# Strassen's scheme for the second projection of a fused retention and snake-activation kernel

## The chip, the cores and the metric

The kernel runs on one core of a Trainium2 chip. A core has five engines that each work through their own queue in order: TensorE (PE; its weight loads are shown apart as PEld), VectorE (DVE), ScalarE (ACT), GpSimd (POOL) and SyncE (SP, which here only issues DMAs). TensorE writes its results to PSUM, which has eight banks; the other operands live in SBUF. The metric is the device time of one execution in microseconds, the median of the runs.

## The reference

Eight batches of retention (attention with a decay instead of a softmax) give 4608 rows of 512 features, and a feed-forward layer with a snake activation maps these rows to the output. Cut to what is computed:

```python
scores = scale * np.matmul(q, k.transpose(0, 1, 3, 2))        # 8 batches, 8 heads, 576 positions, 64 features
ret = scores * Dmat[None, :, :, :]                            # gamma[h] ** (i - j) below the diagonal, 0 above
attn_out = np.matmul(ret, v)
x = attn_out.transpose(0, 2, 1, 3).reshape(B * S, H * D)      # 4608 x 512
h = x @ w_in                                                  # 512 -> 2048
s = np.sin(alpha * h)
g = h + s * s / (alpha + 1e-09)
out = g @ w_out                                               # 2048 -> 512
```

## The kernel before

The 4608 rows are worked on in nine blocks of 512 rows. Blocks 0 to 7 are the first 512 positions of batches 0 to 7; block 8 gathers the last 64 positions of all eight. The output features 2048 of the first projection are cut into sixteen chunks of 128, and a chunk of one block is called a unit here.

One unit (lines 541 to 573): `project(n, u, tag)` runs four matmuls of 128 x 128 x 512 into one PSUM bank `hps`; `sine` (ScalarE) writes `s`; `square` (ScalarE or VectorE, or in a few early places GpSimd) writes `ss`; `product` (VectorE) writes the chunk `gT[n][:, u, :]`, 128 features by 512 rows, in 16-bit floats, and with it the bank is free. In the steady part the banks rotate through three tags, `h0`, `h1` and `h2`, so the projection of unit u + 3 waits for the product of unit u. `gT` has two buffers, one for the block that is being made and one for the block that is being consumed.

The second projection of block n - 1 runs between the units of block n: `gemm2(n - 1, u, tag)` (line 587) is four matmuls of 128 x 128 x 512, that is, 128 of the block's 512 rows against four of the sixteen chunks of `w_out16`. Four such calls fill the bank `op`; `finish` (line 581) copies it to `osb` on ScalarE and stores it with two DMAs from SyncE's queue. A block takes 64 such matmuls.

Blocks 0 to 2 and the beginning of the attention are written out call by call. From line 1140 a loop over n = 3 to 8 writes the order. In each turn of it, called iteration n below, unit u = 0 to 15 does in this order: `project`, `sine`, the calls in `todo[u]`, `square`, `product`, `gemm2`, and the calls in `after[u]`. `at_unit(u, ...)` fills `todo`, `behind(u, ...)` fills `after`. What is placed there is the attention of batch n + 1 (called `A`):

- `scores` at units 3 and 8 into the two double banks `m0` and `m1`, each used twice; `masked` on VectorE behind units 3, 4, 8 and 9 (line 380), which frees the double bank;
- `values` and `add_states` at unit 12, in which the second half of the matmuls waits for a mark that passes through GpSimd's queue (`relay=G_`); `keep` on ScalarE;
- for batch n + 2: loads from SyncE's queue, casts on GpSimd (lines 121 and 194) at units 3 to 8, transposes by DMA from SyncE's queue at units 13 and 15, and the sums of the states (`outer` at unit 12, `chain` on GpSimd).

Iterations 7 and 8 have no such attention; iteration 7 has the small part for block 8 (`Ends`). After the loop, lines 1221 to 1230 run the second projection of block 8: 64 matmuls, of which the last 16 are cut into 320 and 192 columns so that the last copy and store are short.

SBUF is full, so tiles rotate through numbered buffers whose order is written out in the table `BUFFERS`, one digit for each use; `place` takes the next digit.

## Time and profile before

| | us |
|---|---|
| median of 3 runs | 305.76 |
| lowest and highest run | 305.32, 308.21 |
| span of the profiled execution (first to last instruction) | 303.7 |
| TensorE busy in it | 293.0 |
| ScalarE busy | 193.6 |
| VectorE busy | 188.7 |
| GpSimd busy | 136.1 |

The profiled execution's own time is not listed apart from its span; the median of the runs is 2.06 us above the span, and this difference is taken as what lies around it. Iteration n in this text lasts from the start of its first projection to that of the next iteration; the first projections of iterations 4 to 8 start at 136.46, 167.3, 198.2, 228.37 and 258.45 us of the span, and the loop's last matmul ends at about 286.1.

### The profile page before, as it was taken

What the parts mean: (1) busy time and instruction counts of PE and PEld (TensorE: products, weight loads), DVE (VectorE), ACT (ScalarE), POOL (GpSimd) and SP (SyncE); (2) the same over time, 40 slices, a digit from 0 to 9 for tenths busy, and PEclk for the clock granted to TensorE, in tenths of its full rate; (3) what the DMA queues carried; (4) which work ended last, traced back from release to release, by engine and by line L of the source; (5) the groups of instructions that cost most, each with busy time, mean ns of one, the idle gap of its engine ahead of it and who ended that gap; (6) DMA issues with size and microseconds to landing.
All of it is one profiled execution on the core that took longest, in us unless ns stands there. A gap on an engine that the chain in (4) does not pass through costs nothing.

```text
span 303.7 us, 7880 instructions
## 1 busy us (share of the span) xinstructions
PE 293.0 (96%) x3208; PEld 156.8 (52%) x3208; DVE 188.7 (62%) x280; ACT 193.6 (64%) x322; POOL 136.1 (45%) x151
## 2 busy tenths in 40 slices
PE   5899999999989999999999999999999999999995
PEld 4666545645445544554455444544555454444443
DVE  2587876878257776667665666666666755555500
ACT  1569935996776978665776577756764556555411
POOL 4693579482888766587076517743030000000000
PEclk9599999999999999999999999999999999999999
DMA  8999999998798679899788979956451121111232
GB/s 216 349 226 214 259 291 321 227 266 224 169 228 186 149 174 215 236 157 169 166 241 127 183 174 273 171 130 164 103 109 39 41 43 38 37 35 35 47 90 73
DMA packets 120484, 50.05 MB, mean 165 GB/s; under 512 B 80384, under 2 KB 115456, under 8 KB 120448
## 3 DMA queue, kind: packets, MB, share of 16 engines
q1 hardware_dynamic: 116928, 45.17, 63.8%
q0 software_dynamic: 2688, 4.19, 7.6%
q8 instruction: 25, 0.41, 0.5%
q10 hardware_dynamic: 832, 0.18, 0.4%
q14 instruction: 11, 0.09, 0.1%
HBM read 36.75 MB, written 9.44 MB: 152 GB/s over the span
## 4 chain that ended last, share of the span: by engine, by line
PE 84%; DMA 8%; ACT 4%; SPq 1%; issue 1%; POOL 0%; DVE 0%; POOLq 0%; ACTq 0%; DVEq 0%
PE hps L549 38%; PE ops L592 36%; DMA raw<-in_v_dram 5%; PE o L414 3%; PE sc L372 2%; PE kv L308 2%; DMA qT<-q 2%; DMA raw<-in_k_dram 1%; PE o L436 1%; ACT v L119 1%; SPq L143 1%; PE idle L605 1%; ACT kT L119 1%; SPq L585 0%; PE tr L227 0%
## 5 line engine op out<-in xcount | busy, mean ns | idle before, releaser
L573 DVE SCALAR_TENSOR_TENSOR gT<-ss,inva,hps 128x512 f16<-128x512 f16 x144 | 106.1, 746 | 64.0 <-ACT ss L566 59.0
L592 PE MATMUL ops<-w_out,gT 128*128 128x512 f16 (+2 forms) x592 | 142.5, 374 | 0.1
L557 ACT ACTIVATE s<-hps,alpha_t 128x512 f16<-128x512 f32 x144 | 97.5, 684 | 67.3 <-PE hps L549 65.3
L549 PE MATMUL hps<-xT,w_in 128*128 128x512 f16 (+1 forms) x532 | 126.1, 371 | 0.2 <-ACT xT L119 0.2
L549 PEld LDWEIGHTS <-w_in 128*128 128x128 f16 x596 | 66.7, 114 | 57.9 <-DMA w_in<-in_moe_w_in_dram 0.3
L592 PEld LDWEIGHTS <-gT 128*128 128x128 f16 x592 | 56.1, 98 | 62.3 <-issue 0.4
L566 ACT ACTIVATE ss<-s 128x512 f16<-128x512 f16 x73 | 45.9, 631 | 1.4
L568 DVE TENSOR_TENSOR ss<-s 128x512 f16<-128x512 f16 x63 | 32.2, 512 | 19.9 <-ACT s L557 19.4
L194 POOL TENSOR_TENSOR k<-raw,cn 128x1024 f16<-128x1024 f32 (+1 forms) x17 | 29.4, 1733 | 25.9 <-DMA raw<-in_k_dram 25.5
L119 ACT COPY osb<-ops 128x512 f32<-128x512 f32 (+1 forms) x34 | 19.7, 580 | 16.2 <-PE ops L592 14.9
L194 POOL TENSOR_TENSOR q<-raw,cn 128x1024 f16<-128x1024 f32 x13 | 24.6, 1902 | 3.7 <-DMA raw<-in_q_dram 2.7
L384 DVE TENSOR_TENSOR ret<-sc,mask 128x1024 f16<-128x1024 f32 x16 | 19.2, 1221 | 3.0 <-PE sc L372 3.0
L354 POOL TENSOR_TENSOR kvs<-s,kvs 128x256 f32<-128x256 f32 x21 | 16.4, 780 | 4.2 <-ACT kvs L119 1.9
L549 PE MATMUL hps<-xS,w_in 128*128 128x512 f16 x64 | 16.4, 379 | 0.0
L353 POOL TENSOR_TENSOR s<-kvs,cn 128x256 f32<-128x256 f32 x21 | 12.8, 611 | 6.6 <-ACT kvs L119 6.5
L121 POOL CAST v<-raw 128x1024 f16<-128x1024 f32 x10 | 10.5, 1056 | 11.2 <-DMA raw<-in_v_dram 8.5
L384 DVE TENSOR_TENSOR ret<-sc,mask_halved 128x768 f16<-128x768 f32 x16 | 15.2, 951 | 0.0
L178 POOL TENSOR_TENSOR ks<-ks,cn 128x512 f16<-128x512 f32 x4 | 4.2, 1042 | 21.9 <-DMA vs<-in_v_dram 11.6
L119 ACT CAST xT<-o 128x1024 f16<-128x1024 f32 (+1 forms) x15 | 12.9, 878 | 1.1 <-PE o L436 1.0
L346 POOL TENSOR_TENSOR s<-kvs,cn 128x256 f16<-128x256 f32 x17 | 10.8, 635 | 5.8 <-ACT kvs L119 3.4
L372 PEld LDWEIGHTS <-kT 64*64 64x64 f16 x512 | 7.7, 110 | 8.5 <-issue 8.0
L372 PE MATMUL sc<-qT,kT 64*64 64x128 f16 (+1 forms) x512 | 10.7, 219 | 1.2 <-DMA qT<-q 1.1
(58 smaller groups left out, 149.2 us busy)
## 6 DMA issues: line engine op xcount, KB each, us to landing
out_dram<-osb SPq DMA_DIRECT2D x70, 128.0 KB, 2.7
raw<-in_q_dram SPq DMA_DIRECT2D x16, 512.0 KB, 5.4
raw<-in_k_dram SPq DMA_DIRECT2D x8, 512.0 KB, 6.1
raw<-in_v_dram SPq DMA_DIRECT2D x8, 512.0 KB, 7.9
raw<-in_v_dram SPq DMA_DIRECT2D x32, 128.0 KB, 3.0
raw<-in_k_dram SPq DMA_DIRECT2D x32, 128.0 KB, 3.2
w_in<-in_moe_w_in_dram POOLq DMA_DIRECT2D x4, 512.0 KB, 11.5
w_out<-in_moe_w_out_dram POOLq DMA_DIRECT2D x4, 512.0 KB, 12.8
```

The lines of the kernel that those rows point to most:

```text
L119: eng.copy(d_, s_)
L194: eng.tensor_tensor(dst[:, a0:a1].rearrange("p a r t d -> p t (a r) d"), t_.rearrange("p (t a) x -> p t a x", t=2)[:, :, a0:a1].rearrange( ...
L353: nc.gpsimd.tensor_tensor(s32, self.kvs[:, c - 1], g1.unsqueeze(2).to_broadcast([P, 4, D]), MULT)
L354: nc.gpsimd.tensor_tensor(self.kvs[:, c], s32, self.kvs[:, c], ADD)
L372: matmul(sc[halves(g), t, c : c + n], kT[halves(t), 2 * a + r, halves(g)], qT[halves(t), 2 * a : 2 * a + 2, 64 * g + i0 : 64 * g + 64], st ...
L384: nc.vector.tensor_tensor(ret.rearrange("p t (z x) -> p (t z) x", z=2)[:, :, 0:n], sc.rearrange("p t (z x) -> p (t z) x", z=2)[:, :, 0:n], ...
L549: matmul(hps_of[n, fc][0][:, cols], w_in16[fc // 4][:, a, fc % 4 :: 4], xs[n][:, a, cols], start=(a == 0 and part != 1), stop=(a == KT - 1 ...
L557: nc.scalar.activation(s_t, hps, mybir.ActivationFunctionType.Sin, bias=0.0, scale=alpha_t[:, fc : fc + 1],)
L566: nc.scalar.activation(ss_t, s_t, mybir.ActivationFunctionType.Square)
L568: eng.tensor_tensor(ss_t, s_t, s_t, MULT)
L573: nc.vector.scalar_tensor_tensor(gT[n][:, fc, :], ss_t, inva[:, fc : fc + 1], hps, MULT, ADD)
L592: matmul(ops[n, c, cols.start][:, cols], gT[n][:, fk, c * P : (c + 1) * P], w_out16[:, fk, cols], start=(fk == 0), stop=(fk == FC - 1), sk ...
```

## The change

For blocks 3 to 8 the second projection no longer runs as 64 matmuls of 512 columns. The 512 rows are cut into two halves t, the 2048 features into two halves h (chunks 0 to 3 and 8 to 11 for h = 0, the others for h = 1; the index p tells which of the two groups of four chunks), and the 512 output columns into two halves e. Strassen's scheme, in Winograd's form, makes the 2 x 2 product of these quarters from seven products instead of eight. One product (`part_product`) is 16 matmuls of 128 x 128 x 256 into one bank. Their factors are quarters or sums of quarters:

- on the weights, once: `T3`, `T2` and `T4` behind units 5 to 10 of iteration 3, and `T1`, in place in `w_out16`, behind units 2 and 4 of iteration 4, all on VectorE (128 x 1024 each, eight instructions);
- on the rows, for each block: `S3` (in place in `gT`) and `S2` on VectorE, `S1` and `S4` on GpSimd, two halves p of each, 128 x 1024 each. `S3` and `S2` of p = 0 come behind units 11 and 15 of the block's own iteration, those of p = 1 behind units 0 and 1 of the next, and all of `S1` and `S4` behind unit 1 of the next.

The results are put together by ScalarE and VectorE (`after_product`): the first and second product are copied by ScalarE, the five others are added by VectorE to a kept tile (128 x 512, 32 bit) before two stores. Products 2, 7 and 3 accumulate in the bank of products 1, 6 and 5.

The loop's units run in pairs in iterations 4 to 8: both projections of a pair, then one product, with its `after_product` ahead of the second unit's square and product. Iteration 3 keeps the old order (`plain`), since block 2 is still projected as before. Squares are dealt out anew between VectorE and ScalarE, `masked(0, 1)` and the second `scores` move by a unit, casts start one unit later, and two `raw` buffers, and some others, are given to the sums. After the loop, block 8's seven products and eight row sums run in a row.

```diff
@@ BUFFERS
-    "raw": "012345012345012345102405314023140253401253401253",
-    "k16": "0123012302130213",
-    "q16": "0120120121201201",
+    "raw": "012345012345012345102405314023140240124012401240",
+    "k16": "0123012302131313",
+    "q16": "0120120121202020",
...
+    def weight_sum(name, p, eng):
+        b11, b12, b21, b22 = (w_quarter(h, e, p) for h in range(2) for e in range(2))
+        out_, x, y, op = {
+            "T1": lambda: (b12, b12, b11, SUB),
+            "T2": lambda: (piece("T2", p), piece("T3", p), b11, ADD),
+            "T3": lambda: (piece("T3", p), b22, b12, SUB),
+            "T4": lambda: (piece("T4", p), b21, piece("T2", p), SUB),
+        }[name]()
+        eng.tensor_tensor(out_, x, y, op)
+
+    def row_sum(n, name, p, eng):
+        a11, a12, a21, a22 = (quarter(n, t, h, p) for t in range(2) for h in range(2))
+        out_, x, y, op = {
+            "S1": lambda: (piece("S1", p), a11, piece("S2", p), ADD),
+            "S2": lambda: (piece("S2", p), a22, a21, SUB),
+            "S3": lambda: (a21, a11, a21, SUB),
+            "S4": lambda: (piece("S4", p), a12, piece("S2", p), SUB),
+        }[name]()
+        eng.tensor_tensor(out_, x, y, op)
+
+    FACTORS = {
+        1: ((0, 0), (0, 0)), 2: ((0, 1), (1, 0)), 3: ("S4", (1, 1)), 4: ((1, 1), "T4"),
+        5: ("S1", (0, 1)), 6: ("S2", "T2"), 7: ((1, 0), "T3"),
+    }
+
+    def part_product(n, i, tag, js=(0, 1), first=None):
...
+        for j in js:
+            for p in range(2):
...
+                for x in range(4):
+                    matmul(
+                        acc[:, 256 * j : 256 * j + 256], lhs[:, x, 128 * j : 128 * j + 128], rhs[:, x],
...
+    def after_product(n, i, js=(0, 1), issue=(nc.sync, nc.sync)):
+        acc = parts[n, i]
+        if i == 1:
+            nc.scalar.copy(kept_tile("low"), acc)
+        elif i == 6:
+            nc.vector.tensor_tensor(kept_tile("mid"), acc, kept["low"], ADD)
+        elif i == 7:
+            nc.vector.tensor_tensor(kept["low"], acc, kept["low"], ADD)
+        else:
...
+            if i == 2:
+                nc.scalar.copy(osb[:, cols], acc[:, cols])
+            else:
+                nc.vector.tensor_tensor(osb[:, cols], acc[:, cols], kept["mid" if i == 3 else "low"][:, cols], ADD)
+            store(n, t, e, kept[n, i], js, issue)
...
-                behind(4, lambda: A.masked(0, 1))
-                at_unit(8, lambda: A.scores(1, 0, next(m)), lambda: A.scores(1, 1, next(m)))
-                behind(8, lambda: A.masked(1, 0))
+                behind(4 if plain else 5, lambda: A.masked(0, 1))
+                at_unit(late, lambda: A.scores(1, 0, next(m)), lambda: A.scores(1, 1, next(m)))
+                behind(late, lambda: A.masked(1, 0))
...
+                for i, (nm, p) in enumerate((("T3", 0), ("T3", 1), ("T2", 0), ("T2", 1), ("T4", 0), ("T4", 1))):
+                    behind(5 + i, lambda nm=nm, p=p: weight_sum(nm, p, V))
+                behind(11, lambda: row_sum(3, "S3", 0, V))
+                behind(14, lambda: row_sum(3, "S2", 0, V))
+            else:
+                if n < 8:
+                    behind(11, lambda: row_sum(n, "S3", 0, V))
+                    behind(15, lambda: row_sum(n, "S2", 0, V))
+                behind(0, lambda: row_sum(n - 1, "S3", 1, V))
+                behind(1, lambda: row_sum(n - 1, "S2", 1, V))
+                for nm in ("S1", "S4"):
+                    for p in range(2):
+                        behind(1, lambda nm=nm, p=p: row_sum(n - 1, nm, p, G_))
+                if n == 4:
+                    behind(2, lambda: weight_sum("T1", 0, V))
+                    behind(4, lambda: weight_sum("T1", 1, V))
...
+            ON_V = (1, 3, 6, 8, 12, 13) if A else (1, 3, 4, 6, 8, 10, 12, 13)
+            slots = [1, 2, 6, 7, 5, 3, None if A else 4, 4 if A else None]
+            for i in range(8):
+                u = 2 * i
+                unit_start(u)
+                unit_end(u, V if u in ON_V else A_)
+                unit_start(u + 1)
+                if slots[i] is not None:
+                    k_ = slots[i]
+                    part_product(n - 1, k_, None if k_ in (2, 7, 3) else "op", first={2: 1, 7: 6, 3: 5}.get(k_))
+                    after_product(n - 1, k_)
+                unit_end(u + 1, V if u + 1 in ON_V else A_)
+        n = NBLK - 1
+        part_product(n, 4, next(h))
+        part_product(n, 1, "op")
+        after_product(n, 1)
+        for p in range(2):
+            row_sum(n, "S3", p, V)
+            row_sum(n, "S2", p, V)
+        row_sum(n, "S1", 0, G_)
+        row_sum(n, "S1", 1, V)
+        row_sum(n, "S4", 0, G_)
+        row_sum(n, "S4", 1, V)
+        part_product(n, 6, next(h))
+        after_product(n, 6)
+        part_product(n, 2, None, first=1)
+        after_product(n, 2)
+        part_product(n, 7, None, first=6)
+        after_product(n, 7)
+        after_product(n, 4)
+        part_product(n, 5, next(h))
+        after_product(n, 5)
+        for j in range(2):
+            part_product(n, 3, None, (j,), first=5)
+            after_product(n, 3, (j,), (nc.sync, nc.scalar))
```

Here `quarter` and `w_quarter` are views of `gT` and `w_out16`, `piece` gives a sum's tile, `unit_start(u)` is `project`, `sine` and `todo[u]`, and `unit_end(u, eng)` is `square` on `eng`, `product` and `after[u]`.

151 lines of the change are left out of this document (104 added, 47 removed).

## The prediction

> **What bounds the kernel now.** First the page's busy shares and the granted clock, then a table of the stages (one row for each iteration 3 to 8 and the tail, cut at the first projection of each block), then the last pieces of the chain that ended last.
>
> ```profile
> span 303.7 us, 7880 instructions
> ...
> PE 293.0 (96%) x3208; PEld 156.8 (52%) x3208; DVE 188.7 (62%) x280; ACT 193.6 (64%) x322; POOL 136.1 (45%) x151
> ...
> PEclk9599999999999999999999999999999999999999
> ```
>
> ```profile
> core 0: us, PE busy (x) PEld busy (x) DVE busy (x) ACT busy (x) POOL busy (x), PEclk, DMA share, GB/s
> 105.55:136.46 30.91, 30.91 (x346) 15.87 (x345) 21.01 (x31) 22.56 (x39) 20.52 (x26) 1.00 0.89 193
> 136.46:167.30 30.84, 30.84 (x346) 15.86 (x345) 19.53 (x27) 20.96 (x34) 17.97 (x19) 1.00 0.86 176
> 167.30:198.20 30.90, 30.90 (x346) 15.94 (x345) 19.86 (x27) 20.98 (x34) 17.17 (x18) 1.00 0.95 195
> 198.20:228.37 30.17, 30.17 (x282) 15.16 (x281) 18.95 (x27) 20.06 (x32) 8.42 (x10) 1.00 0.55 127
> 228.37:258.45 30.08, 30.01 (x321) 15.18 (x320) 18.97 (x30) 16.81 (x29) 0.00 (x0) 1.00 0.19 41
> 258.45:286.10 27.65, 27.65 (x130) 13.46 (x129) 16.71 (x28) 15.03 (x25) 0.00 (x0) 1.00 0.17 39
> 286.10:303.70 17.60, 14.00 (x81) 7.49 (x79) 1.11 (x2) 3.36 (x7) 0.00 (x0) 1.00 0.32 76
> ```
>
> ```profile
> 283.65 0.86 PE ops L592 x4
> 284.52 0.86 PE hps L549 x4
> 285.38 14.73 PE ops L592 x84
> ...
> 300.19 0.36 DVE osb L121
> ```
>
> In iterations 4 to 8 TensorE is busy for the whole of each row at full clock; VectorE stands at about 19.5 of 30.9 us. So a matmul less is time saved, as long as TensorE still finds its operands and banks ready. The last copy ends at 300.55, so the tail (from the loop's end at 286.10) is 14.45 us. The five iterations 4 to 8 and the tail make 30.84 + 30.90 + 30.17 + 30.08 + 27.65 + 14.45 = 164.1 us.
>
> **The matmuls: what goes.** Four matmuls of 512 columns take 0.86 us, 0.216 each, so a block's 64 take 13.8. A matmul of 256 columns isn't in this stage; the tail's cut ones, 320 and 192 columns, bound it:
>
> ```profile
> 296.71 3.38 PE L592 MATMUL ops<-w_out,gT 128*128 128x320 f16 x30
> ```
>
> ```profile
> L592 PE MATMUL ops<-w_out,gT 128*128 128x512 f16 x560 | 139.0, 379 | 0.1
> ...
> L592 PEld LDWEIGHTS <-gT 128*128 128x128 f16 x592 | 56.1, 98 | 62.3 <-issue 0.4
> ```
>
> In the first row the last 30 matmuls, 14 of 320 and 16 of 192 columns (the row shows the form of the first), take 3.38 us. Less the drain of the last (0.379 − 0.216 = 0.16) that is 3.22 us for 7552 columns, 0.426 ns a column; the uncut ones have 0.422. So a matmul of 256 columns takes 0.109 us, a product of 16 takes 1.75, and seven take 12.2: 1.6 us less per block, 8.0 in iterations 4 to 8. The weight load of 98 ns hides under 192 columns (0.082 us) already, so it is no bound here. The Trainium skill speaks against that step: the page "TensorE: Matmul & The Clock Gate", section "Back-to-back issue gap", gives 81 ns at 128 and 131 ns at 512 columns for streams of load and matmul, an estimate of 98 ns at 256, by which 112 narrow matmuls would cost 2.6 us more than 64 wide ones. This trace, with 216 ns at 512 columns, doesn't agree.
>
> **What comes on VectorE.**
>
> ```profile
> L573 DVE SCALAR_TENSOR_TENSOR gT<-ss,inva,hps 128x512 f16<-128x512 f16 x144 | 106.1, 746 | 64.0 <-ACT ss L566 59.0 <-POOL ss L568 2.3
> L557 ACT ACTIVATE s<-hps,alpha_t 128x512 f16<-128x512 f32 x144 | 97.5, 684 | 67.3 <-PE hps L549 65.3 <-DVE ret L384 1.5
> ...
> L566 ACT ACTIVATE ss<-s 128x512 f16<-128x512 f16 x73 | 45.9, 631 | 1.4
> ...
> L384 DVE TENSOR_TENSOR ret<-sc,mask_halved 128x768 f16<-128x768 f32 x16 | 15.2, 951 | 0.0
> ...
> L568 POOL TENSOR_TENSOR ss<-s 128x512 f16<-128x512 f16 x8 | 8.2, 1039 | 7.0 <-ACT s L557 6.9
> ...
> L121 DVE COPY osb<-ops 128x512 f32<-128x512 f32 x2 | 1.4, 687 | 2.3 <-PE ops L592 2.3
> ...
> L121 DVE COPY kT<-tr 128x512 f16<-128x512 f16 x2 | 0.8, 420 | 0.6 <-PE tr L227 0.6
> ...
> L121 DVE COPY kT<-tr 128x1024 f16<-128x1024 f16 x1 | 0.7, 684 | 0.0
> ```
>
> Five adds of 512 elements in 32 bits per block: the nearest row is the copy of such a bank, 0.69 each, 3.4 in all. A sum of 128 x 1024 in 16 bits: a 512-wide 16-bit copy takes 420 ns and the 1024-wide one 684; the square, which has two inputs in SBUF as the sums have, takes 0.42 at 512 (below), so 0.68 alone; four per block are 2.7. One square less is −0.4. VectorE in iteration 5 goes from 19.9 to 25.6 us, in iteration 4, with the two halves of T1, from 19.5 to 26.6. ScalarE loses two copies per block and gains a square; it stays off the path. On GpSimd a sum of 1024 is twice the 1039 ns row: about 1.95, four per block 7.8, which makes 17.97 into 25.8 us of a 29.2 us iteration 4.
>
> **Collisions.** A 16-bit operation with two SBUF inputs waits on VectorE while GpSimd works:
>
> ```profile
> 134.79 0.43 DVE L568 TENSOR_TENSOR ss<-s 128x512 f16<-128x512 f16 x1 [0.92 <-ACT s L557]
> ...
> 139.47 1.90 POOL L194 TENSOR_TENSOR k<-raw,cn 128x1024 f16<-128x1024 f32 x1
> ...
> 139.97 1.68 DVE L568 TENSOR_TENSOR ss<-s 128x512 f16<-128x512 f16 x1
> ...
> 141.31 1.23 POOL L121 CAST v<-raw 128x1024 f16<-128x1024 f32 x1
> ```
>
> ```profile
> 170.17 1.91 POOL L194 TENSOR_TENSOR k<-raw,cn 128x1024 f16<-128x1024 f32 x1 [1.58 <-DMA raw<-in_k_dram]
> 170.80 1.55 DVE L568 TENSOR_TENSOR ss<-s 128x512 f16<-128x512 f16 x1 [0.23 <-ACT s L557]
> ```
>
> The squares at 139.97 and 170.80 end 0.3 us after GpSimd's operation, wherever they started. So one such operation costs 0 to 1.3 us extra. Before, GpSimd idles in the middle of the iterations:
>
> ```profile
> 151.19 1.90 POOL L194 TENSOR_TENSOR k<-raw,cn 128x1024 f16<-128x1024 f32 x1 [8.65 <-DMA raw<-in_k_dram]
> ```
>
> Exactly this gap is filled by S1 and S4. Iteration 4 has twelve such operations on VectorE (six squares, four row sums, two of T1); at 0.5 each, between 0 and 1.3 and near what a GpSimd busy for 88% in pieces of 1.9 us leaves on average, they add 6 us: 32.6 of 29.2. The Trainium skill, page "SBUF — State Buffer", section "Who interferes with whom", has the pair of ports locked for the whole instruction, but only against VectorE operations with two SBUF inputs, or in a two-port mode. By it the five adds, with one input in PSUM, go free; were they to wait too, at 0.5 each, that would be 2.5 us more per iteration. The products' even 746 ns beside GpSimd speak for the rule.
>
> **The order of iteration 4, step by step** (us from its start; P is a projection of 0.86, F a product of 1.75, numbers as in the diff). P0, P1 and F1 end at 3.5. S3 of p = 1 meets GpSimd's first S1 (3.0 to 5.0) and ends at 5.5; square 1 6.0, product 1 6.7, S2 7.4, product 2 8.1. T1 waits for the second S1 and ends at 9.9, square 3 waits for S4 and ends at 11.9, product 3 at 12.6. P6 takes product 3's bank and could have begun at 10.9: 1.8 us of stall. Mask 13.5, product 4 14.3; T1's second half waits for a cast, 16.0; add 6 16.7, product 5 17.5, mask(0,1) 18.4. P7 loses 0.9 on product 4, and `scores(1,1)` needs mask(0,1)'s bank: 3.0 more. With 0.5 for product 13 behind the chain's small operations the walk gives 29.2 + 6.1 = 35.3 us. Queued behind the waiting sum on VectorE are always the next product, and behind that the bank of a projection three units on.
>
> The same walk gives 31.8 in iteration 5 (no T1), 30.4 in 6, 30.2 in 7 and 26.75 in 8. Without collisions they would take TensorE's 29.3, 28.6, 28.5 and 26.05, the first two with 0.7 for `scores(1,1)`: mask(0,1) ends an add, a product and a mask (0.17 + 0.69 + 0.75 + 0.95 = 2.6) after F6, and TensorE is there after two projections and half the scores, 1.9. Iteration 4, where VectorE's sum is past TensorE's, is taken as walked; for the others I take the middle: 30.9, 29.85, 29.35, 26.4. Iteration 3 gets eight sums on VectorE (21.0 + 5.5 + some 3 of collisions, of 30.9); walked against its slack of 2 us per bank it stalls nowhere: 0.
>
> **The tail.** No product stands behind the last pair of units, so product 15 comes 2.75 us after P15 (sine 14, square 14, sine 15 and square 15 on ScalarE, then 0.75), and the eighth matmul of F4 waits for it: F4 ends at 3.85, F1 at 5.6. The four sums S3 and S2 begin on VectorE at 2.75 and end at 5.5 alone; then F6 7.4, F2 9.15, F7 10.9, F5 12.65, 0.9 for the add before F3 can write its bank, F3 15.35, last add 15.9. If GpSimd's S1 gets in between S3 and S2, and S4 before the next, 18.2. The middle, 17.05, is 2.6 us over the 14.45 of before.
>
> **Sum.** 35.3 + 30.9 + 29.85 + 29.35 + 26.4 + 17.05 = 168.85, 4.75 over 164.1. On the profiled execution 308.45; with the 2.06 between span and median, 310.5, 1.6% slower. Stores stay at two DMAs of 128 KB each, in rows half as long. Fewer `raw` buffers cost nothing as long as SyncE's queue runs late anyway (the load behind the 8.65 us wait above); the loads for q wait for a cast that ends before their turn.
>
> **Rivals.**
> 1. Faster (0.23). The sums fall into GpSimd's gaps, or get the port first. The point is iteration 4: with under 0.2 us of collision per operation VectorE stays at 26.6 + 2.4 < 29.2. Then 29.9 + 30.0 + 29.3 + 28.5 + 26.05 + 15.9 = 159.65, −4.45: 301.3. For it: VectorE's sum alone fits. Against: the two rows of 1.68 and 1.55.
> 2. Cancelled (0.20). Half the stalls: within 1%, 304 to 308.
> 3. Slower still (0.15). The walk everywhere (35.3 + 31.8 + 30.4 + 30.2 + 26.75 + 18.2 = 172.65, +8.55, 314.3), or GpSimd, 88% busy, brings casts and the relay mark late at unit 13. Against the latter: its 8.65 us of idle time exceed the 7.8 added.
> 4. The narrow matmuls cost their loads in full (0.02): 0.109 + 0.098, 23.2 per block, past 350; the 30 matmuls above exclude it nearly.
>
> **How the numbers follow.** Forecast 0.40, rivals as above. A change under 1% can't be told from none here. Faster by over 1%: 0.23; within: 0.20; slower: 0.57. The range runs from below rival 1 to rival 3's walk: 300.5 to 315.
>
> **What would show it.** Right: iteration 4 at 33 us or more, squares and sums of VectorE that end 0.3 us after GpSimd's, TensorE idle behind products 3 to 5 and mask(0,1), a tail of 16 to 18 us. Wrong: iterations at 28.5 to 29.5 with TensorE full, sums at an even 0.68, or GpSimd's sums far from 1.95.

## The result and the profile after

The changed kernel takes 319.15 us in the median (316.81 to 320.19) against 305.87 for the kernel before (305.32 to 308.21) beside it: 1.039 times as long, with an interval of 1.0325 to 1.0456. It is slower, as forecast, but by 13.3 us and not by 4.75, and it lies 4 us above the range. Ratios and intervals, here and in the table further down, leave out executions more than 1.5% above the kernel's fastest, and the profiled execution of a2_no_gpsimd_sums (318.75 us) is one of these.

The profiled execution took 316.81 us, the lowest of the runs, with a span of 315.1 us against 303.7. The table of stages of the changed kernel, cut as before: rows for iterations 4 to 8, then one from the loop's end to the end of the span. Columns: length, busy time of each engine with its instructions, granted clock (the share of its full clock that TensorE was given), DMA.

```profile
core 0: us, PE busy (x) PEld busy (x) DVE busy (x) ACT busy (x) POOL busy (x), PEclk, DMA share, GB/s
136.34:172.23 35.89, 31.23 (x394) 20.95 (x393) 30.69 (x35) 20.49 (x33) 25.22 (x19) 0.95 0.72 144
172.23:204.83 32.60, 30.02 (x395) 20.65 (x393) 30.20 (x36) 21.96 (x35) 28.79 (x24) 1.00 0.87 191
204.83:234.89 30.06, 28.98 (x330) 19.99 (x329) 26.93 (x35) 19.11 (x29) 18.66 (x16) 1.00 0.65 131
234.89:263.81 28.92, 28.60 (x371) 19.77 (x369) 23.97 (x36) 17.66 (x29) 8.78 (x4) 1.00 0.19 43
263.81:291.75 27.94, 26.57 (x176) 18.17 (x177) 23.54 (x32) 16.45 (x26) 8.77 (x4) 1.00 0.16 38
291.75:315.10 23.35, 13.55 (x113) 10.64 (x111) 12.71 (x15) 3.03 (x6) 4.96 (x2) 0.98 0.23 57
```

Against before, TensorE no longer fills its rows: 4.7 us of iteration 4 and 2.6 of iteration 5 are idle. The differences are +5.05 (iteration 4), +1.7, −0.1, −1.2 and +0.3, then +4.0 in the tail (18.49 from the loop's end to the last add at 310.24, against 14.45) and +1.7 behind the last add (4.86 against 3.15): 11.4 us, the whole difference of the spans. Of this, nearly half is in one iteration.

What the row sums (line 640) cost, GpSimd's first and then VectorE's S3; the columns are least, median and largest duration in ns:

```profile
L640 POOL TENSOR_TENSOR S<-gT,S x22: 2117/2297/2569, 139.5 to 298.4; 128x1024 f16<-128x1024 f16 x22
L640 DVE TENSOR_TENSOR gT<-gT x12: 683/793/2610, 129.8 to 295.8; 128x1024 f16<-128x1024 f16 x12
```

And iteration 4, from the timeline; the bracket is the idle time before the row and what ended it:

```profile
139.53 2.13 POOL L640 TENSOR_TENSOR S<-gT,S 128x1024 f16<-128x1024 f16 x1
139.59 2.61 DVE L640 TENSOR_TENSOR gT<-gT 128x1024 f16<-128x1024 f16 x1
...
144.06 6.91 POOL L640 TENSOR_TENSOR S<-gT,S 128x1024 f16<-128x1024 f16 x3 [2.41 <-PE ops L659]
...
144.50 2.24 DVE L630 TENSOR_TENSOR w_out<-w_out 128x1024 f16<-128x1024 f16 x1
...
146.66 2.33 DVE L569 TENSOR_TENSOR ss<-s 128x512 f16<-128x512 f16 x1
...
149.83 1.34 PE L550 MATMUL hps<-xT,w_in 128*128 128x512 f16 x4 [2.33 <-DVE gT L574]
...
151.22 2.17 DVE L630 TENSOR_TENSOR w_out<-w_out 128x1024 f16<-128x1024 f16 x1
...
155.56 0.37 PE L373 MATMUL sc<-qT,kT 64*64 64x128 f16 x16 [1.88 <-DVE ret L385]
```

The first row sum starts 0.06 us after GpSimd's S1 and ends 0.54 us after it: 2.61 us for work whose shortest row is 0.68. T1's first half (line 630) and the square behind it stand beside GpSimd's three sums in a row, 144.06 to 150.97, and take 4.6 us together instead of 1.1. Product 3 comes late for that, and TensorE waits 2.33 us for its bank.

The two rows that show a second loss, from a finer table of the same view (the last three columns are granted clock, DMA share, GB/s):

```profile
145.00:150.00 5.00, 2.67 (x21) 1.96 (x20) 4.96 (x4) 2.45 (x4) 5.00 (x3) 1.00 0.67 152
150.00:155.00 5.00, 3.50 (x24) 1.23 (x23) 5.00 (x6) 2.00 (x3) 5.00 (x4) 0.66 0.78 190
```

Behind the gap the granted clock is at half for 3.41 us (150.4 to 153.8 in the record of the clock), and the four matmuls of the projection at 149.83 take 1.34 us where others take 1.03.

The tail, from the chain of the work that ended last:

```profile
296.56 2.43 DVE S L640
298.99 0.02 issue
299.01 1.57 DVE S L640
300.58 0.85 issue
301.43 0.68 DVE S L640
302.11 0.61 DVE mid L691
...
307.20 1.05 PE ops L659 x8
...
308.27 0.44 DVE osb L703
...
308.75 1.05 PE ops L659 x8
...
309.82 0.42 DVE osb L703
```

From 296.56 to 302.72 the chain is on VectorE: three sums, held or waiting, and the add of `mid`. Then at the end the second half of the last product (308.75) waits for the add of the first half (308.27), though it writes the other half of the bank. Finally SyncE's queue, in its own timeline:

```profile
302.92 9.66 SPq L670 DMA_DIRECT2D out_dram<-osb  x14
```

Fourteen stores are issued until 312.58, 2.3 us after the last add. Block 8's branch of `store` issues one DMA per j and r, so four of 64 KB for a quarter.

### The profile page after: what moved, and what is told of

Same layout as the page of the kernel before. It is cut to its first block, busy times and chain, and to the rows that moved or that the text cites. A ratio compares the mean times of both kernels' runs of the same rounds, so it can differ in the third digit from the quotient of the medians.

```text
span 315.1 us, 8517 instructions
## 1 busy us (share of the span) xinstructions
PE 288.3 (91%) x3480; PEld 183.6 (58%) x3480; DVE 247.5 (79%) x333; ACT 195.1 (62%) x321; POOL 188.5 (60%) x173
## 4 chain that ended last, share of the span: by engine, by line
PE 47%; DVE 25%; DMA 13%; ACT 6%; issue 3%; SPq 2%; POOL 2%; POOLq 0%; DVEq 0%; ACTq 0%
PE hps L550 24%; PE ops L659 12%; PE ops L593 7%; DVE gT L574 7%; DVE ss L569 5%; DMA raw<-in_k_dram 4%; DMA raw<-in_v_dram 4%; DVE S L640 4%; DVE gT L640 3%; DMA w_in<-in_moe_w_in_dram 3%; ACT s L558 2%; DVE ret L385 2%; ACT ss L567 2%; DMA qT<-q 1%; PE o L415 1%
## 5 line engine op out<-in xcount | busy, mean ns | idle before, releaser
L550 PE MATMUL hps<-xT,w_in 128*128 128x512 f16 (+1 forms) x532 | 123.3, 374 | 5.3 <-DVE gT L574 4.8
L640 POOL TENSOR_TENSOR S<-gT,S 128x1024 f16<-128x1024 f16 x22 | 49.1, 2252 | 49.8 <-DVE S L640 42.0
L567 ACT ACTIVATE ss<-s 128x512 f16<-128x512 f16 x84 | 52.7, 630 | 2.3
L593 PE MATMUL ops<-w_out,gT 128*128 128x512 f16 x192 | 46.8, 380 | 0.0
L659 PEld LDWEIGHTS <-gT 128*128 128x128 f16 x384 | 36.8, 98 | 10.2 <-DVE gT L574 1.8
L569 DVE TENSOR_TENSOR ss<-s 128x512 f16<-128x512 f16 x52 | 38.1, 735 | 5.2 <-ACT s L558 5.2
L659 PEld LDWEIGHTS <-S 128*128 128x128 f16 x288 | 28.0, 98 | 9.2 <-issue 1.6
L593 PEld LDWEIGHTS <-gT 128*128 128x128 f16 x192 | 17.9, 98 | 20.4
L659 PE MATMUL ops<-T,gT 128*128 128x256 f16 x192 | 23.3, 273 | 2.0 <-DVE gT L574 1.5
L659 PE MATMUL ops<-w_out,S 128*128 128x256 f16 x192 | 23.1, 273 | 1.3 <-DVE osb L703 1.3
L659 PE MATMUL ops<-w_out,gT 128*128 128x256 f16 x192 | 23.0, 273 | 0.0
L373 PE MATMUL sc<-qT,kT 64*64 64x128 f16 (+1 forms) x512 | 11.4, 222 | 4.7 <-DVE ret L385 3.5
```

The lines of the kernel that those rows point to most:

```text
L550: matmul(hps_of[n, fc][0][:, cols], w_in16[fc // 4][:, a, fc % 4 :: 4], xs[n][:, a, cols], start=(a == 0 and part != 1), stop=(a == KT - 1 ...
L567: nc.scalar.activation(ss_t, s_t, mybir.ActivationFunctionType.Square)
L569: eng.tensor_tensor(ss_t, s_t, s_t, MULT)
L593: matmul(ops[n, c, cols.start][:, cols], gT[n][:, fk, c * P : (c + 1) * P], w_out16[:, fk, cols], start=(fk == 0), stop=(fk == FC - 1), sk ...
L640: eng.tensor_tensor(out_, x, y, op)
L659: matmul(acc[:, 256 * j : 256 * j + 256], lhs[:, x, 128 * j : 128 * j + 128], rhs[:, x], start=(tag is not None and j == 0 and p == 0 and ...
```

## The experiments

All lengths of the profiled executions in one table, in us, by the same cuts ("end" is from the last add or copy to the end of the span; "half clock" the time at half clock in iterations 4 and 5). The ratio is that of each kernel to the kernel before as it ran beside it. Their edits, expectations and readings follow.

| kernel | it. 4 | it. 5 | it. 6 | it. 7 | it. 8 | tail | end | half clock | median | ratio to before, interval |
|---|---|---|---|---|---|---|---|---|---|---|
| before | 30.84 | 30.90 | 30.17 | 30.08 | 27.65 | 14.45 | 3.15 | 0 | 305.87 | |
| changed | 35.89 | 32.60 | 30.06 | 28.92 | 27.94 | 18.49 | 4.86 | 3.41 | 319.15 | 1.0391, 1.0325 to 1.0456 |
| a2_no_gpsimd_sums | 36.80 | 31.89 | 29.12 | 28.72 | 26.36 | 18.42 | 4.8 | 3.41 | 315.24 | 1.0308, 1.0240 to 1.0377 |
| a3_no_vector_sums | 37.15 | 30.39 | 29.09 | 30.42 | 26.06 | 18.49 | 4.9 | 6.83 | 317.20 | 1.0389, 1.0291 to 1.0487 |
| a4_squares_on_scalar | 35.89 | 31.60 | 29.10 | 28.55 | 26.70 | 18.49 | 4.8 | 3.41 | 314.17 | 1.0240, 1.0132 to 1.0348 |
| a8_gpsimd_memsets | 36.81 | 33.82 | 29.10 | 28.74 | 26.36 | 18.42 | 4.8 | 10.24 | 315.47 | 1.0329, 1.0204 to 1.0455 |
| a5_old_tail | 36.86 | 31.92 | 30.06 | 28.92 | 27.93 | 14.80 | 3.2 | 6.83 | 314.49 | 1.0280, 1.0222 to 1.0339 |
| a6_merged_stores | 38.27 | 32.78 | 30.04 | 28.91 | 27.93 | 18.49 | 3.35 | 10.24 | 317.86 | 1.0406, 1.0355 to 1.0457 |
| a10_no_gpsimd_sums_at_all | 30.63 | 31.62 | 29.09 | 28.73 | 26.35 | 18.43 | 4.86 | 0 | 309.17 | 1.0129, 1.0070 to 1.0188 |
| b2_blocks_6_7 | 30.83 | 30.89 | 30.19 | 28.59 | 26.05 | 14.47 | 3.36 | 0 | 302.82 | 0.9915, 0.9876 to 0.9955 |
| a9_no_T1 | 30.89 | 32.55 | 30.20 | 28.92 | 27.94 | 18.49 | 4.8 | 0 | 313.25 | 1.0186, 1.0127 to 1.0246 |
| a12_tail_sums_on_vector | 37.04 | 32.12 | 30.08 | 28.90 | 27.95 | 16.48 | 4.81 | 3.41 | 315.78 | 1.0294, 1.0230 to 1.0358 |
| a13_no_tail_sums | 37.17 | 32.22 | 30.06 | 28.92 | 27.94 | 16.48 | 4.88 | 6.83 | 315.22 | 1.0262, 1.0188 to 1.0337 |
| a14_no_gpsimd_squares_scalar | 32.13 | 31.65 | 29.10 | 28.56 | 26.71 | 18.42 | 4.87 | 0 | 310.58 | 1.0118, 1.0051 to 1.0184 |

### Is it the collision? One partner taken away at a time

The theory: VectorE's two-input operations and GpSimd's sums hold each other up. The rival: the sums are too much work for their engine, each by itself. Four kernels leave T1 and block 3's sums in iteration 4 as they are. Three of them act on the sums of blocks 4 to 7, and one on the squares of iterations 4 to 8.

GpSimd's S1 and S4 left out:

```diff
-                for nm in ("S1", "S4"):
+                for nm in ("S1", "S4") if n == 4 else ():
```

> Leaves out the sums S1 and S4 on GpSimd for blocks 4 to 7 (block 3's stay, and its values are used again, so the output of these blocks is not the reference's); the tail is as in the changed kernel. Lengths of iterations 4 to 8 in the changed kernel: 35.9, 32.6, 30.1, 28.9, 27.9 us. Theory (collisions: VectorE's operations with two SBUF inputs wait for GpSimd's): iteration 4 stays, 5 falls to 30.6, 6 to 29.4, 7 to 28.6, 8 to 26.3; the span falls from 315.1 by 4 to 5 us, to about 310.5. Rival (VectorE's plain work and the order of its queue): VectorE has the same instructions as before, so iterations 5 to 8 stay within 0.5 us and the span at 314 to 315.

VectorE's S2 and S3 left out:

```diff
-                if n < 8:
-                    behind(11, lambda: row_sum(n, "S3", 0, V))
-                    behind(15, lambda: row_sum(n, "S2", 0, V))
-                behind(0, lambda: row_sum(n - 1, "S3", 1, V))
-                behind(1, lambda: row_sum(n - 1, "S2", 1, V))
+                if n == 4:
+                    behind(0, lambda: row_sum(n - 1, "S3", 1, V))
+                    behind(1, lambda: row_sum(n - 1, "S2", 1, V))
```

> Leaves out the sums S2 and S3 on VectorE for blocks 4 to 7 (block 3's stay; the output of these blocks is not the reference's). Theory (collisions): the squares on VectorE still meet S1 and S4 on GpSimd; iteration 5 falls to about 31.3, 6 to 29.6, 7 to 28.7, 8 to 27.3; the span to about 312.5. Rival (plain work): four sums are 2.7 us less of VectorE per iteration, more than the stalls of iterations 6 to 8 and most of that of 5; the span falls by 4 us or more, to 311 or less.

All squares of iterations 4 to 8 on ScalarE, nothing left out:

```diff
-            ON_V = (1, 3, 6, 8, 12, 13) if A else (1, 3, 4, 6, 8, 10, 12, 13)
+            ON_V = ()
```

> Puts all squares of iterations 4 to 8 on ScalarE (six or eight more per iteration, 0.63 each, on an engine that is busy for 20.5 of 35.9 us in iteration 4). Theory (collisions): with six of ten or twelve operations that can collide gone, iteration 4 falls to 34, 5 to 30.8, 6 to 29.6, 8 to 26.6; the span to about 310.5. Rival (plain work): VectorE loses 0.42 per square, 2.5 us per iteration, and no waits; if this were all, the span would fall by 1 to 2 us, and squares on ScalarE behind a copy that waits for TensorE could make it slower.

S1 and S4 replaced by work on GpSimd that reads nothing:

```diff
-                        behind(1, lambda nm=nm, p=p: row_sum(n - 1, nm, p, G_))
+                        if n == 4:
+                            behind(1, lambda nm=nm, p=p: row_sum(n - 1, nm, p, G_))
+                        else:
+                            behind(1, lambda nm=nm, p=p: G_.memset(piece(nm, p), 0.25))
+                            behind(1, lambda nm=nm, p=p: G_.memset(piece(nm, p), 0.25))
```

> Replaces each sum S1 and S4 on GpSimd for blocks 4 to 7 by two memsets of the same tile, so GpSimd is busy at the same places but reads nothing from SBUF (the output of these blocks is not the reference's). Theory, with the Trainium skill's page SBUF - State Buffer, section Who interferes with whom (only GpSimd operations that read SBUF hold up a VectorE operation with two SBUF inputs): squares and sums beside the memsets last 0.42 and 0.68 us, and the span is that of the kernel without these sums, about 310.5. Rival (any GpSimd operation holds VectorE up, or its being busy at all): waits as in the changed kernel, the span above 313.

The spans (317.0, 317.2, 312.5 and 315.5 us) are 2 to 6.5 us above what the theory expected, and the last is even where its rival put it (above 313). But in these executions iteration 5 begins 1.0 to 5.6 us later than in the changed kernel, so what lies ahead of it hides the gain. Iterations 5 to 8 decide. They take 119.5 us together in the changed kernel and 116.1, 116.0, 116.0 and 118.0 in these four (the last with half clock in iteration 5). Without GpSimd's sums VectorE has the same instructions as in the changed kernel, so the rival asked for at most 0.5 us of change in each iteration, and 3.4 us went in all. The run without VectorE's sums decides nothing by its sum: 3.6 us lie between the theory's 2.6 and the rival's 4.

Iterations 6 and 8 answer alike, whichever partner goes: 30.06 becomes 29.1 in all four, 27.94 becomes 26.1 to 26.7. Iteration 7 falls to 28.55 to 28.74 in three of them. Without VectorE's sums it is 30.42, and the timeline of that kernel shows why:

```profile
262.24 4.39 POOL L640 TENSOR_TENSOR S<-gT,S 128x1024 f16<-128x1024 f16 x2 [3.19 <-DVE gT L574]
262.30 2.34 DVE L569 TENSOR_TENSOR ss<-s 128x512 f16<-128x512 f16 x1 [0.24 <-ACT s L558]
```

GpSimd's sums of block 7 no longer wait for S2, so three of them run in iteration 7 already, where they hold the squares at its end (2.34 and 0.96 us instead of 0.42), and TensorE waits 1.7 us there. So this edit moved GpSimd's work as well. Taking away VectorE's own work, GpSimd's, or only the squares, shortens iterations 6 and 8 alike, which speaks for the pair and against either engine's load. The last kernel shows the cause at the operation, in its timeline in iteration 6:

```profile
211.18 0.68 DVE L640 TENSOR_TENSOR gT<-gT 128x1024 f16<-128x1024 f16 x1
211.63 0.95 POOL L1314 MEMSET S<- 128x1024 f16 x1
211.78 0.42 DVE L569 TENSOR_TENSOR ss<-s 128x512 f16<-128x512 f16 x1
212.52 0.95 POOL L1313 MEMSET S<- 128x1024 f16 x1
212.90 0.69 DVE L640 TENSOR_TENSOR S<-gT 128x1024 f16<-128x1024 f16 x1
```

In this iteration GpSimd is nearly as busy as in the changed kernel (17.3 against 18.7 us), and VectorE's square and sums take their undisturbed 0.42 and 0.68 us; so do all 13 squares and sums of iterations 5 to 8 that ran beside nothing but memsets. (The memsets wait for no sum and run early, so in iteration 8 GpSimd is idle, and only iterations 6 and 7 are a comparison at like load.) The Trainium skill, page "SBUF — State Buffer", section "Who interferes with whom", says that a VectorE instruction with two SBUF inputs contends with a GpSimd instruction that reads SBUF, and not with one that only writes it. The trace agrees.

Iteration 5 answers otherwise: only without VectorE's sums does it fall below before (30.39); 31.6 to 31.9 remain without GpSimd's or without the squares on VectorE, and 33.8 in the run with memsets, which had a window of half clock there.

### Iteration 4: GpSimd's sums, or T1?

Iteration 4 got shorter in none of these four (35.89 to 37.15), not even with its squares on ScalarE, where 34 was expected and 35.89 came. Two more take its own parts away: in one all of GpSimd's sums are replaced by memsets, block 3's too; in the other T1 goes.

```diff
-                        behind(1, lambda nm=nm, p=p: row_sum(n - 1, nm, p, G_))
+                        behind(1, lambda nm=nm, p=p: G_.memset(piece(nm, p), 0.25))
```

> S1 and S4 left out for all blocks that iterations 4 to 8 project, block 3 too (a memset of a constant in place of each, so products 3 and 5 are wrong in value and the same in size). The run without GpSimd's sums had them still in iteration 4. If iteration 4's 35.9 us come from GpSimd's four sums of block 3, which hold VectorE's sums, T1 and squares up (an excess of 8.4 us over 12 operations), then T1 takes 0.7 an operation and not 2.2, product 3's wait and the wait of scores on the mask go, no window of half clock follows, and iteration 4 takes 29.3 to 31. The rival, that the order of the work on VectorE (T1, the row sums, the masks and squares on one queue) is too long by itself whatever GpSimd does: iteration 4 stays above 33. Iterations 5 to 8 as in the run without GpSimd's sums: 31.9, 29.1, 28.7, 26.4; the tail 18.4.

```diff
-                    behind(2, lambda: weight_sum("T1", 0, V))
-                    behind(4, lambda: weight_sum("T1", 1, V))
+                    pass
```

> The changed kernel with the two VectorE operations of T1 in iteration 4 left out (product 5 then multiplies by the old quarter and is wrong in value). They took 2.2 us each there, beside GpSimd's sums, and 0.7 each in the run without these. If T1 is one operation among those that GpSimd's sums hold up, the held time passes to the next ones: VectorE's queue gets shorter by T1's own 1.4 us and part of the 3.0 that it was held, and iteration 4, 35.9 us, takes 33 to 35 (with one window of half clock at most). The rival, that T1 itself is what iteration 4 cannot take and GpSimd's sums only lengthen it: iteration 4 falls to 31. Iterations 5 to 8 and the tail as in the changed kernel (32.6, 30.1, 28.9, 27.9, 18.5).

Iteration 4 in the table of stages, first without GpSimd's sums, then, in a fence of its own, without T1:

```profile
136.68:167.31 30.63, 29.42 (x393) 20.70 (x392) 24.02 (x35) 20.52 (x34) 19.87 (x19) 1.00 0.88 167
```

```profile
137.32:168.21 30.89, 29.74 (x394) 20.69 (x392) 26.95 (x33) 20.51 (x34) 24.27 (x19) 1.00 0.73 159
```

Either removal takes the whole 5 us away. For GpSimd's sums that was the theory's expectation. For T1 the theory said 33 to 35, with the held time passing to the next operations. That was wrong: the rival's 31 came. So the loss needs both. T1's halves are 1.4 us of work; the first meets GpSimd's three sums in a row and the second, so delayed, GpSimd's next operation, and they take 4.4 us. Moving the squares away leaves exactly these two held (2.24 and 2.52 us in that kernel), which is why it didn't help. With T1 or the sums gone, the longest wait of TensorE in iteration 4 is 0.8 or 1.2 us, and the clock stays whole. With the sums gone the kernel is at 309.17, 10 us under the changed one.

### The rest of iteration 5: squares beside the casts?

Without any of GpSimd's sums iteration 5 still takes 31.6. Its long rows, from the timeline of that kernel (no GpSimd sum in it):

```profile
189.81 4.21 POOL L195 TENSOR_TENSOR q<-raw,cn 128x1024 f16<-128x1024 f32 x2 [3.00 <-DMA raw<-in_q_dram]
...
192.18 2.12 DVE L569 TENSOR_TENSOR ss<-s 128x512 f16<-128x512 f16 x1
...
195.13 1.02 PE L550 MATMUL hps<-xT,w_in 128*128 128x512 f16 x4 [1.46 <-DVE gT L574]
```

A square stands behind GpSimd's casts of q, which the kernel before has as well. So this kernel was run with all squares on ScalarE too (`ON_V = ()`):

> The run without any of GpSimd's sums (a memset in place of each of S1 and S4) with all squares of iterations 4 to 8 on ScalarE as well. Without GpSimd's sums iteration 5 still took 31.6 us, and its one long row was a square on VectorE of 2.05 beside GpSimd's cast of q (4.21 us for two), with a wait of 1.46 on TensorE behind it. If that is the rest of iteration 5's loss, it takes 29.0 to 29.6 now, as iterations 6 and 7 do, and iteration 4 (30.6, with one such square of 2.06 on the path) 29.2 to 30. The rival, that VectorE's own row sums are too much work for iterations that also have the masks: both stay above 30.3. Iterations 6 to 8: 29.1, 28.6, 26.4; tail 18.4.

It missed: iteration 5 stays at 31.65 and iteration 4 rises to 32.13. The chain of the work that ended last, in iteration 4 of that kernel, says why:

```profile
162.94 0.30 ACT kvs L120
...
163.43 1.02 ACT xT L120
164.44 0.11 ACT kvs L120
164.55 0.26 issue
164.81 0.66 ACT ss L567
```

Behind unit 13 ScalarE evicts the attention's banks (kvs, xT), and the square now queues there; product and projection follow it. In iteration 5 of this kernel the same chain (kvs, xT, the square, the product) ends in its one long wait of TensorE, 1.66 us at 197.95. So the square left the casts and met the evictions, and the run doesn't tell what the casts alone cost. The place is tight for whichever engine has the square. That VectorE's own sums are the rest of iteration 5's loss is supported by the one run without them (30.39), but it was not tried alone with clean clocks; it stays open.

### The tail and the end

Block 8 as before the change (64 wide matmuls, ScalarE's copies, eight stores):

```diff
-        n = NBLK - 1
-        part_product(n, 4, next(h))
...
+        for c in range(3):
+            tag = next(h)
+            for u in range(4 * c, 4 * c + 4):
+                gemm2(NBLK - 1, u, tag)
+            finish(NBLK - 1, c)
```

> The changed kernel with one part undone: block 8, behind the loop, is projected by the 64 matmuls of 512 columns, the ScalarE copies and the eight stores of the kernel before; two VectorE adds in iteration 8 put the quarter that T1 overwrote back (b12 = T1 + b11). Blocks 3 to 7 stay with seven products. If the tail's own cost is what the trace of the changed kernel shows (18.5 us from the loop's end to the last add against 14.45, and 4.9 against 3.2 us from there to the end), the tail is 14.4 to 14.6 and the profiled execution 5.5 to 5.9 us shorter than 315.1, some 309.4; the median falls by about as much, to 313.5. The rival, that block 8's stores and not its sums set the end: the tail is back, but the end gains less than 4.5. Iterations 4 to 7 do not move; iteration 8 takes the two adds and may lose up to 0.7.

The tail's matmuls and its last copy, in the timeline of that kernel:

```profile
296.44 14.02 PE L593 MATMUL ops<-w_out,gT 128*128 128x512 f16 x80 [0.17 <-DVE gT L574]
...
310.55 0.36 DVE L122 COPY osb<-ops 128x192 f32<-128x192 f32 x1 [11.73 <-PE ops L593]
```

From the loop's end (296.11) to 310.91 are 14.8 us, and the end is 3.2: 5.35 less than 18.49 + 4.86, a little under the 5.5 to 5.9 expected (the tail itself was expected at 14.4 to 14.6). The median fell by 4.7; the span by only 1.0, since in this profiled execution iteration 3 began 2.95 us later, iterations 3 and 4 took 1.1 and 1.0 longer, and iteration 5 took 0.7 less. The two adds in iteration 8 cost nothing (27.93).

Only block 8's stores merged:

```diff
-                for j in js:
-                    issue[r].dma_start(rows_of(n, 2 * t + j)[r, :, cols], osb[halves(r), j])
+                dst = out.rearrange("(u j r s) d -> u r s j d", u=2, j=2, r=2)
+                issue[r].dma_start(dst[t, r, 512:576, js[0] : js[-1] + 1, cols], osb[halves(r), js[0] : js[-1] + 1])
```

> The changed kernel with the output stores of block 8 merged: each store of a quarter is one DMA for both j (two a quarter, where the changed kernel issues four), the halves of the last quarter as before. If SP's queue of fourteen issues, which ends 2.3 us after the last add, is what lengthened the end, then the time from the last add to the end falls from 4.9 to about 3.2 us, and the time by 1.5 to 1.8. If the end is set by the landing of the last half alone, whatever stands ahead of it in the queue, it moves by less than 0.3. Iterations 4 to 8 and the tail up to the last add (18.5) do not move.

SyncE's queue in its timeline (last add here: 312.33 to 312.75):

```profile
305.43 7.84 SPq L670 DMA_DIRECT2D out_dram<-osb  x8
```

Eight issues end 0.5 us after the last add instead of 2.3, and the end is 3.35 us instead of 4.86: −1.5, as expected. The median (317.86) fell by 1.3, less than the two medians can tell apart; this reading rests on the trace.

The tail's sums all on VectorE, and left out:

```diff
-        row_sum(n, "S1", 0, G_)
-        row_sum(n, "S1", 1, V)
-        row_sum(n, "S4", 0, G_)
-        row_sum(n, "S4", 1, V)
+        for nm in ("S1", "S4"):
+            for p in range(2):
+                row_sum(n, nm, p, V)
```

> The changed kernel with all eight row sums of block 8, behind the loop, on VectorE (S1 and S4 of half 0 there too, in place of GpSimd). In the trace of the changed kernel the three VectorE sums beside GpSimd's two take 2.43, 1.57 and 0.68 us with 0.85 of waiting, and mid's add ends 302.72 where the first of them started 296.56. Eight sums of 0.68 on one engine: from 296.56 on five sums, 3.4, mid's add at 299.96 and its end at 300.6, 2.1 us earlier; product 7 and all behind it follow, and the tail is 16.2 to 16.6 instead of 18.5, the time 2 us less for equal clock. The rival, that the tail is set by the exits (adds after products 4, 5 and 3 and the split halves) and the sums are hidden: less than 0.7 us.

> The changed kernel with the row sums of block 8, behind the loop, left out (its products 3, 5, 6 and 7 take what the pieces and quarters hold, wrong in value and the same in size). What is left of the tail are seven products of 1.75 us, 12.25, the wait for the last gT and the exits. If the sums are what the tail lost (4.0 us over the 14.45 of the kernel before), it takes 14 to 15.5: seven products start as early as the 64 matmuls (13.8) did and end 1.6 earlier, but the last quarter leaves in two halves with an add between, 1.1. The rival, that the chain of adds (low, mid, low, four outputs) sets it: above 16.5.

Both tails are 16.48 us, for the first as expected (16.2 to 16.6). With all eight sums on VectorE the chain is TensorE's from the last product on:

```profile
294.77 0.76 DVE gT L574
295.53 0.05 issue
295.57 9.90 PE ops L659 x89
```

So GpSimd's two sums in the tail cost 2.0 us and VectorE's eight nothing. The other 2.0 us over 14.45 are in neither, and there the theory (14 to 15.5 without sums) missed. Beside the tail by wide matmuls (14.8) the 16.48 are made up so: the 112 narrow matmuls save their 1.6 us (12.4 against 14.0); TensorE waits 1.95 us for the last gT, after seven matmuls of product 4, where the wide ones started 0.33 after the loop's end; and the exits outside the matmuls, two adds in series after product 5 and after the first half of product 3, and the last, are 2.06 us against 0.45. Two losses of 1.6 against one gain of 1.6.

### Only where it pays

The runs put the gain of the products (1.5 to 1.6 us a block where nothing is held) beside three costs: GpSimd's sums, the iterations with masks, and the tail. A kernel without these: from the kernel before, seven products for blocks 6 and 7 alone, weight sums on VectorE in iteration 6, T1 in a tile of its own, row sums on VectorE, most squares on ScalarE, and some of block 8's small attention part moved to later units of iteration 7.

```diff
+            if n == 6:
+                for u, (nm, p) in zip((1, 2, 5, 6, 7, 10, 11, 12), ((nm, p) for nm in ("T3", "T2", "T4", "T1") for p in range(2))):
+                    behind(u, lambda nm=nm, p=p: weight_sum(nm, p, V))
+            if n in (6, 7):
+                behind(13, lambda: row_sum(n, "S3", 0, V))
+                behind(15, lambda: row_sum(n, "S2", 0, V))
+            if n >= 7:
+                for u, (nm, p) in enumerate((("S3", 1), ("S2", 1), ("S1", 0), ("S1", 1), ("S4", 0), ("S4", 1))):
+                    after.setdefault(u, []).insert(0, lambda nm=nm, p=p: row_sum(n - 1, nm, p, V))
...
```

> The kernel before, with seven products of quarters for blocks 6 and 7 alone, in iterations 7 and 8, where no masked chunk is computed beside them: all weight sums (T1 in a tile of its own) on VectorE in iteration 6, where the causal work is over as well; all row sums on VectorE and none on GpSimd; most squares on ScalarE; block 8 as in the kernel before. If what costs the changed kernel its gain is the holding up of VectorE by GpSimd, the causal iterations and the tail, and the seven products themselves save 1.6 us a block, then iterations 4 and 5 stay at 30.8 and 30.9, iteration 6 at 30.1 to 30.6, iteration 7 takes 28.4 to 28.9 (from 30.1), iteration 8 26.1 to 26.6 (from 27.65), the tail 14.45, and the time is 2 to 3 us under the kernel before, 302.7 to 304. The rival, that VectorE's row sums by themselves cost what the products save: within 1 us of the kernel before.

Its iterations 6 to 8 in the table of stages, and then the durations of its row sums (line 639 there):

```profile
198.04:228.23 30.19, 30.19 (x281) 15.20 (x280) 24.22 (x36) 20.09 (x32) 8.86 (x10) 1.00 0.53 121
228.23:256.82 28.59, 28.55 (x369) 19.95 (x368) 22.69 (x36) 20.56 (x36) 0.00 (x0) 1.00 0.20 46
256.82:281.99 25.17, 25.17 (x170) 17.37 (x169) 20.32 (x33) 17.93 (x29) 0.00 (x0) 1.00 0.16 39
```

```profile
L639 DVE TENSOR_TENSOR S<-gT,S x8: 681/684/686, 236.9 to 268.9; 128x1024 f16<-128x1024 f16 x8
```

GpSimd does nothing in iterations 7 and 8, every row sum takes 0.68, TensorE is full, and iteration 7 is 1.5 us shorter, iteration 8 (with the half product behind its last projection, to 282.87) 1.6. The time is 302.82, 0.9915 of before with an interval of 0.9876 to 0.9955. So it is faster than the kernel before by 0.85%, a small difference, but one whose interval excludes 1; beside the changed kernel's median it is 5% less. The rival, no gain for VectorE's sums, is out by the rows of iterations 7 and 8.

## Why the prediction was right or wrong

**The matmuls: right.** Products of 16 take 1.75 us in every chain (1.05 for 8 with their drain), and 1.5 to 1.6 us a block are saved where TensorE is full. The rival of narrow matmuls is out.

**VectorE's adds: right,** 0.69 each, also beside GpSimd. VectorE's sums alone are 0.68, as taken.

**GpSimd's sum: mis-sized.** Forecast 1.95; least 2.12, median 2.30. It is held up by VectorE in its turn, but even its shortest is over the doubled row of 1039 ns.

**Collisions: right mechanism, mis-sized where they come in rows.** The prediction's rows of squares, 0.3 us past GpSimd's end, were carried over to sums of twice the width; those end 0.55 past it. And GpSimd's sums come in rows, so a held operation mostly waits for a whole one. Excess over the undisturbed durations, worked out over squares, row sums and T1: 8.35 us over 12 operations in iteration 4 (0.70 each), 7.3 over 10, 4.5 over 10, 1.5 over 12 and 4.2 over 11 in iterations 5 to 8. Over all 55 that is 0.47, so the 0.5 that was taken is about the mean, and too small for iterations 4 and 5 (0.70 and 0.73).

**The walk of iteration 4: near the measurement partly by chance.** 35.3 forecast, 35.89 measured. The stall on product 3 was put at 1.8 and is 2.33, that of `scores(1,1)` at 3.0 and is 1.88, that on product 4 at 0.9 and is 0.18. TensorE idles 4.7 us in all, where the walk has 6.1 (its own four terms add up to 6.2). Against that stands the half clock, for which the prediction has no term: 1.5 to 1.8 us (TensorE busy 31.23, against 29.74 without T1 and 29.42 without GpSimd's sums, both at full clock). "Take away GpSimd's sums" and "take away T1" show that the walk had the right two causes.

**"For the others I take the middle": the step that failed first.** The walk itself said 31.8, 30.4, 30.2 and 26.75; measured 32.6, 30.06, 28.92 and 27.94. Iterations 6 and 7 are within 0.4 of the middle (29.85, 29.35), iterations 5 and 8 are above even the walk: +1.7 and +1.5 against the forecast (30.9, 26.4). The halving had no reason that named which collisions would not happen, and they did: in iteration 5 eight of ten operations were held (7.3 us), and in iteration 8 two squares beside a row of three GpSimd sums took 2.00 and 1.56 us, with 1.2 us of TensorE's waiting behind them. The tail was halved in the same way, 17.05 between 15.9 and 18.2, and is 18.49. Its lower end, 15.9, had no add between the two halves of the last product (0.5); without any sums the tail is 16.48. The walk's upper end, GpSimd's sums between VectorE's, is what occurs, plus that add. Halving for iterations 5 to 8 and the tail makes 4.4 of the 6.7 us that the forecast of the span lacked.

**"Stores stay at two DMAs of 128 KB each": wrong for block 8,** whose branch issues four of 64 KB. That is 1.5 to 1.7 us behind the last add.

**Iteration 3 at 0: right in this execution** (30.86), but it took 30.85 to 31.99 in the twelve kernels that have these weight sums (the changed one among them), and so it costs up to 1.1.

Measured against forecast, in span: +0.6, +1.7, +0.2, −0.4, +1.5, tail +1.4, end +1.7, together 6.7: 315.1 against 308.4. The median lies another 2 us higher than the profiled execution puts it, and this one had the highest mean clock of the four (0.993; the others 0.984, 0.980 and 0.978, with spans of 317.0, 317.9 and 318.5). The prediction has no term for the clock. That these 2 us are more half clock fits the order of the four; only one of them has a trace, so it isn't shown. The rival nearest to the result is the third, "the walk everywhere", 314.3; with the stores it would have been 316.

## What to carry to other kernels

A product saved on the busiest engine is worth its time only in stages where the additions that pay for it cost nothing; price each stage by itself, and leave the change out of those that lose. In these traces VectorE and GpSimd were not two independent engines: a VectorE operation with two SBUF inputs that started beside a running GpSimd operation that reads SBUF ended only after it. So price such work on VectorE alone, if it fits there. When a walk through the order gives a number for a stage, halve it only for a reason that names which collision doesn't happen.

## What the runs showed of the hardware

**In iteration 4 a gap of TensorE cost twice.** The granted clock falls to half for 3.41 us (or a multiple) behind stretches in which TensorE waits. One such window in iteration 4 adds 1.5 to 1.8 us to TensorE's busy time. Among the changed kernel and the four whose iteration 4 is the same, one window goes with 35.89 and 37.04 us (TensorE idles 4.7 and 5.7 us there), two with 36.86 and 37.17, and three with 38.27. Cut each trace into stretches of 3.41 us, in step with its own record of the clock. Between 20 us and the loop's end of all fourteen traces, every stretch in which TensorE was busy for 1.50 us or less was followed by half clock (1.08 us in the changed kernel, 0.57 to 1.50 in the others), and no stretch at full clock with 1.67 us or more was. Where half clock lasted longer than one stretch, TensorE was busy for 1.6 to 2.5 us of each such stretch but the last. No single wait in iteration 4 was longer than 2.9 us, and where the longest was 1.8 us or less (without T1, and in the two kernels without any of GpSimd's sums) no half clock came. The Trainium skill, page "TensorE: Matmul & The Clock Gate", section "What's actually happening", has the same free-running window of 3413 ns, but the half clock only after an idle one; here a window that was busy for a third (1.08 of 3.41 us) was enough. Where the gap falls in the window differs from one execution to the next, which is likely why the changed kernel's runs spread; that was not tested apart.

**A held VectorE operation does nearly all its work after GpSimd's end.** In the changed kernel the held sums of 1024 end 0.55 us after the GpSimd sum in whose time they started, and the held squares of 512 0.28 us, whenever they started: their undisturbed 0.68 and 0.42 less 0.13 or 0.14. GpSimd's casts hold them in the same way (T1's second half ends 0.55 us after one). GpSimd's next sum is held in its turn, 2.57 or 2.30 instead of 2.12. So a row of GpSimd sums let through one two-input VectorE operation per sum, and both engines paid.
